# One load of the query weights becomes five strided loads on the sync engine's queue, with the small inputs behind them

## The chip, the core and the metric

The kernel runs on one core of a Trainium2 chip. The core has a matrix engine (PE, its weight loads shown as PEld), a vector engine (DVE), a scalar engine (ACT), GpSimd (POOL) and a sync engine (SP), and sixteen DMA engines that all transfers share. SP and ACT each issue transfers on a queue of their own. The metric is device time in microseconds (us), the median of several executions; lower is better.

## The reference

One decoding step of a transformer layer, two sequences (B = 2), one new token each, width D = 512:

- layer norm of x, then q = norm(x) @ wq, split into H = 32 heads of 128;
- attention of each of the 64 pairs (sequence, head) over 8192 cached keys and values: `softmax(q k^T / sqrt(128)) v`, all in float32;
- the heads' outputs times wo (4096 x 512), added to x;
- a second layer norm, `relu(. @ w1 + b1)**2 @ w2 + b2` with 1792 hidden columns, added again.

The 64 blocks of keys and values are 8.39 MB each and make up 537 of the 561 MB that are read. The query weights wq are another 8.39 MB, wo is 8.39 MB, w1 and w2 are 3.67 MB each. The small inputs (x, b1, b2) are 13 KB.

## The kernel before

All inputs are laid out on the host so that a load is one contiguous row for each of the 128 partitions. The on-chip memory holds `ring`, three slots of 128 partitions x 16384 float32, 64 KB a partition and 8.39 MB a slot. A key and value block fills one slot. Slot 2 first takes the query weights, and later wo; slot 0 takes w1 and w2 at the end.

**Opening.** ACT issues the load of the small inputs into `sm` (line 200) on its own queue; SP issues the query weights into slot 2 (line 201) and then key and value blocks 0 and 1 into slots 0 and 1 (lines 202 and 203). DVE and PE compute the layer norm from `sm` (the reduction `part` at line 253, then `xc`, `rstd`, `xn` up to line 258). PE multiplies `xn` by the weights (lines 269 to 274), `big` is turned and scaled into `QT` (lines 276 to 282), and the first queries are spread into `q3` and `QR`. When PE has read the weights, SP issues block 2 into slot 2 (line 287).

**Loop.** Lines 306 to 313 are SP's loop: for each block, wait until a slot is free, then issue the next load into it. Lines 315 to 350 are the loop of PE, DVE and ACT over blocks 0 to 59: scores on PE, maximum on DVE, exponentials on ACT, four weighted sums on DVE, after which the slot is free.

**Tail.** The last four blocks, wo, w1, w2, the projection and the second half of the layer follow in straight code. The last instruction of weight is the store of `out` (line 591).

**What sets the order.** Outside the loop every operation is recorded by the class `Line` with the memory that it reads and writes, and `plan()` works out which semaphores it must wait for. Three rules of it matter here. First, `region()` (lines 51 to 60) describes an access by the tensor's name and the range of elements *within a partition*; it leaves out which partitions are touched:

```python
lo = ap.offset % row
hi = lo + 1 + sum(step * (n - 1) for step, n in ap.ap[1:])
```

Second, in `plan()` (lines 69 to 80) two accesses conflict when their ranges overlap and one of them is a write. A conflict is passed over when the earlier one has the same engine as `source`, but a load is entered under a name of its own, `("load", n)`, and not under `"sp"`:

```python
if l < hi and lo < h and (w or write):
    if source == engine and (engine == "pe" or not w):
        continue
    needs[source] = max(needs.get(source, 0), n)
```

Third, an operation that needs a load waits on its engine's queue until that load's semaphore has reached 16 (`flush()`, line 118), and what the engine has to issue behind it stands behind that wait. A load issued by SP also waits for the load eight before it (`AHEAD`).

The blocks 0, 1 and 2 are issued by plain operations, which `plan()` doesn't see as writes of the first two slots.

Of the kernel before, what the change touches and what calls it, by code (L numbers as in the profile page):

```python
# [167 lines left out]
def attention_block_kernel(nc, small, kvd, wqd, wod, w1d, w2d, out):  # L168
    def sb(name, *shape):
        return nc.alloc_sbuf_tensor(name, [P, *shape], F32).ap()  # L170

    line = Line(nc)
    pe, dve, act, sp = nc.tensor, nc.vector, nc.scalar, nc.sync
# [5 lines left out]
    ring = sb("ring", SLOTS, ROW)  # L179
# [16 lines left out]
    sm = sb("sm", DB * B + FB + DB)  # L196
    xT = sm[:, : DB * B].rearrange("p (a b) -> p a b", b=B)
    b1T = sm[:, DB * B : DB * B + FB]
    b2T = sm[:, DB * B + FB :]
    line.load(sm, small, "act")  # L200
    line.load(ring[:, 2], wqd)
    for i in range(2):
        line.op("sp", lambda e, i=i: e.dma_start(slot(i), kvd[i]).then_inc(kv_full[i], 16))
    line.op("sp", lambda e: e.sem_inc(s_free, 2))
# [420 lines left out]
```

## Time and profile before

| what | value |
|---|---|
| median of 3 runs (lowest, highest) | 1304.16 us (1303.73, 1304.47) |
| the profiled execution: its time, its span | 1303.86 us, 1302.2 us |
| read from HBM | 561.00 MB, 431 GB/s over the span |
| DVE, PE, ACT busy | 740.4, 417.2, 144.9 us |
| DMA issue of the query weights, to landing | at 0.75 us, 21.9 us |
| DMA issue of the small inputs, to landing | at 0.74 us, 22.1 us |
| first reduction of the small inputs on DVE | at 22.86 us |
| issue of blocks 0 and 1; of block 2 | from 1.20 us; at 35.09 us |

The span is the time from the first to the last instruction; the profiled execution's time is 1.66 us more. A transfer has two times: its issue, an instruction of some 0.4 us on the issuing engine, and its landing, when its semaphore is complete. In the views of transfers a packet is what one DMA engine moves at a stretch; here it is one partition's row of 64 KB, and a slice that shows 9 is one in which packets begin, the whole of a packet being counted where it begins.

### The profile page before, as it was taken

How to read it: one execution, taken by the hardware profiler on the slowest of the kernel's cores; microseconds unless marked ns; L12 is line 12 of the kernel's file. 1: busy time of each engine (PE TensorE's matmuls, PEld its weight loads, DVE VectorE, ACT ScalarE, POOL GpSimd, SP SyncE). 2: the span in 40 equal slices, each digit the busy share in tenths (PEclk: the TensorE clock that was granted, in tenths of full speed). 3: DMA queues.
4: the chain of work that ended last, by engine and by line, in shares of the span. 5: the costliest groups of instructions: out<-in, count | busy, mean ns of one | idle time of the engine just before them, and what ended most of it. 6: DMA issues, size and time to landing. Idle time of an engine off the chain costs nothing. (4 is left out here: it accounts for less than half of the span.)

```text
span 1302.2 us, 6730 instructions
## 1 busy us (share of the span) xinstructions
PE 417.2 (32%) x2438; PEld 112.1 (9%) x2438; DVE 740.4 (57%) x709; ACT 144.9 (11%) x152; POOL 0.7 (0%) x6
## 2 busy tenths in 40 slices
PE   2323223313313313313323323322322332332546
PEld 0100000000000000000000000000000000000112
DVE  0365655665564665665565565665566466556564
ACT  1010111011011011011011011011101001101111
POOL 0000000000000000000000000000000000000000
PEclk9666667566666667666556556656656656655778
DMA  9999999999999999999999999999999999999998
GB/s 419 420 445 425 445 425 443 425 437 433 431 437 427 443 423 445 425 443 427 443 425 435 435 429 439 423 445 425 445 425 443 425 439 431 433 435 427 428 429 367
DMA packets 12104, 561.18 MB, mean 431 GB/s; under 512 B 1472, under 2 KB 1600, under 8 KB 2880
## 3 DMA queue, kind: packets, MB, share of 16 engines
q1 hardware_dynamic: 11952, 561.06, 99.7%
q8 instruction: 5, 0.08, 0.0%
q10 hardware_dynamic: 144, 0.01, 0.0%
q14 instruction: 3, 0.02, 0.0%
HBM read 561.00 MB, written 0.07 MB: 431 GB/s over the span
## 5 line engine op out<-in xcount | busy, mean ns | idle before, releaser
L345 DVE SCALAR_TENSOR_TENSOR ring<-ring,s 128x2048 f32<-128x2048 f32 x240 | 534.7, 2284 | 136.3 <-DVEq L299 136.3
L328 PE MATMUL s<-ring,q 128*32 128x512 f32 x1920 | 354.5, 906 | 800.2 <-PEq L299 800.2
L334 DVE TENSOR_REDUCE st<-s 128x1 f32<-128x2048 f32 x60 | 137.5, 2292 | 330.6 <-DVEq L299 330.6
L340 ACT ACTIVATE s<-s,st 128x2048 f32<-128x2048 f32 x60 | 116.5, 1942 | 1037.1 <-ACTq L299 1037.1
L328 PEld LDWEIGHTS s<-ring,q 128*32 128x32 f32 x1920 | 88.9, 158 | 1064.8 <-issue 1064.8
L155 DVE SCALAR_TENSOR_TENSOR ring<-ring,s 128x2048 f32<-128x2048 f32 x15 | 33.7, 2283 | 6.8 <-ACT s L137 6.8
L133 PE MATMUL s<-ring,QR 128*32 128x512 f32 x128 | 22.1, 851 | 31.4 <-DMA ring<-in_kvd 25.0
L159 DVE TENSOR_REDUCE ALL<-s 128x1 f32<-128x2048 f32 x4 | 9.2, 2292 | 19.2 <-PE s L133 19.2
L345 DVE DVE_READ_ACCUMULATOR ring<-ring,s 128x1 f32 x240 | 19.9, 83 | 0.0
L349 DVE TENSOR_SCALAR ALL<-st 128x6 f32 x60 | 10.3, 171 | 15.1 <-DVEq L299 15.1
L137 ACT ACTIVATE s<-s,ALL 128x2048 f32<-128x2048 f32 x4 | 7.8, 1942 | 49.6 <-DVE ALL L159 49.6
L159 DVE TENSOR_REDUCE part<-sm 128x2 f32<-128x8 f32 x1 | 0.2, 160 | 21.8 <-DMA sm<-in_small 21.8
L340 ACT ACTIVATION_READ_ACCUMULATOR s<-s,st 128x1 f32 x60 | 11.6, 193 | 0.0
L133 PE MATMUL s<-ring,OT 128*2 128x512 f32 (+1 forms) x70 | 9.7, 684 | 3.6 <-DMA ring<-in_wod 3.6
L133 PE MATMUL s<-part,ones_d 128*128 128x2 f32 x8 | 2.1, 332 | 24.2 <-DVE part L159 24.2
L133 PE MATMUL s<-ring,xn 128*2 128x512 f32 x64 | 9.4, 751 | 0.8 <-DVE xn L147 0.8
L133 PEld LDWEIGHTS s<-ring,QR 128*32 128x32 f32 x128 | 4.9, 150 | 47.3 <-DMA ring<-in_kvd 27.0
L133 PE MATMUL s<-lw,pick_all 128*128 128x32 f32 (+2 forms) x6 | 1.9, 395 | 13.7 <-DVE lw L147 13.7
L151 DVE TENSOR_SCALAR QT<-s 128x64 f32<-128x64 f32 x1 | 0.2, 225 | 10.6 <-PE s L133 10.6
L137 ACT ACT_TABLE_LOAD x4 | 5.1, 1283 | 1.2 <-PEq L618 1.2
L133 PE MATMUL s<-ring,xc 128*2 128x448 f32 x32 | 5.0, 739 | 0.4 <-DVE xc L147 0.3
L133 PE MATMUL s<-ring,a 128*2 128x128 f32 x112 | 4.0, 272 | 3.8 <-DMA ring<-in_w2d 3.7
(73 smaller groups left out, 57.5 us busy)
## 6 DMA issues: line engine op xcount, KB each, us to landing
ring<-in_kvd SPq DMA_DIRECT2D x3, 4096.0 KB, 32.6
ring<-in_wod SPq DMA_DIRECT2D x1, 4096.0 KB, 27.5
ring<-in_w1d SPq DMA_DIRECT2D x4, 896.0 KB, 21.5
ring<-in_kvd SPq DMA_DIRECT2D x1, 3072.0 KB, 28.7
ring<-in_wod SPq DMA_DIRECT2D x1, 2048.0 KB, 33.2
ring<-in_w2d SPq DMA_DIRECT2D x2, 1024.0 KB, 15.6
ring<-in_wod SPq DMA_DIRECT2D x1, 1536.0 KB, 36.4
ring<-in_kvd SPq DMA_DIRECT2D x2, 512.0 KB, 37.5
```

The source lines that it names most:

```text
L133: self.op("pe", lambda e: e.matmul(out, lhsT, rhs, start=start, stop=stop), [lhsT, rhs], [out])
L137: self.op("act", lambda e: e.activation(out, in_, func, bias=bias, scale=scale, accum_out=accum_out), [in_, *more], [out] + ([] if accum_o ...
L151: self.op("dve", lambda e: e.tensor_scalar(out, in_, by, None, op0=ALU.mult), [in_, *more], [out])
L155: self.op("dve", lambda e: e.scalar_tensor_tensor(out, a, by, b, op0=op0, op1=op1, accum_out=accum_out), [a, b, *more], [out] + ([] if acc ...
L159: self.op("dve", lambda e: e.tensor_reduce(out, in_, axis=AX.X, op=op, negate=negate), [in_], [out])
L328: made = pe.matmul(bk[n][32 * j : 32 * j + 32, :], q3[:, u, :], keys(u)[:, j, n * BLK : (n + 1) * BLK], start=True, stop=True)
L334: dve.tensor_reduce(nm, s, axis=AX.X, op=ALU.max, negate=True).then_inc(m_full, 1)
L340: act.activation(s, s, AF.Exp, bias=nm, scale=1.0, accum_out=ls).then_inc(e_full, 1)
L345: made = dve.scalar_tensor_tensor(v, v, 1.0, s, op0=ALU.mult, op1=ALU.mult, accum_out=st3[:, u, 2 + e : 3 + e])
L349: dve.tensor_scalar(ALL[:, bass.ds(i0 + u, 1)], st3[:, u : u + 1], 1.0, None, op0=ALU.mult).then_inc(kv_free, 1)
```

## The change

The small inputs are no longer issued by ACT but by SP, behind the query weights. The query weights are no longer one load of 128 partitions but five: partitions 0, 8, 16, ... (16 of them), partitions 4, 12, 20, ... (16), and then three loads of 32 partitions that begin at 1, 2 and 3 and go in steps of 4. Together they are the same 128 rows of 64 KB. Everything else stays.

```diff
-    line.load(sm, small, "act")
-    line.load(ring[:, 2], wqd)
+    for lo, step in ((0, 8), (4, 8), (1, 4), (2, 4), (3, 4)):
+        line.load(ring[lo::step, 2], wqd[lo::step])
+    line.load(sm, small)
     for i in range(2):
         line.op("sp", lambda e, i=i: e.dma_start(slot(i), kvd[i]).then_inc(kv_full[i], 16))
     line.op("sp", lambda e: e.sem_inc(s_free, 2))
```

In the built program the second to the fifth of these loads each carry a wait for the load before them; the load of the small inputs and those of blocks 0 and 1 carry none. PE's first product with the weights waits for the fifth load.

## The prediction

> **What bounds the kernel now.** I read the page's first lines, then busy time and transfers by stretch:
>
> ```profile
> 0.00:22.40 22.40, 0.00 (x0) 0.00 (x0) 0.18 (x3) 3.68 (x4) 0.70 (x6) 1.00 1.01 422
> 22.40:100.00 77.60, 29.12 (x180) 8.81 (x180) 35.69 (x43) 9.12 (x11) 0.00 (x0) 0.71 1.00 430
> 500.00:700.00 200.00, 59.67 (x320) 14.89 (x320) 117.70 (x108) 20.58 (x20) 0.00 (x0) 0.61 1.00 435
> 1278.50:1302.20 23.70, 15.31 (x208) 7.01 (x204) 6.72 (x24) 2.22 (x5) 0.00 (x0) 0.90 0.86 351
> ```
>
> The last two columns are the DMA engines' busy share and GB/s. From the first microseconds to 1278.5 us the share is 1.00, while DVE, the busiest engine, works 118 of 200 us. The transfers bound the kernel, so idle time put into their stream near the start moves everything behind it by as much. The loop can't take it back by waiting less, because SP already waits for slots, in the wait view:
>
> ```profile
> SPq L299 <- SPq L299: 1128.8, 60, 27.3
> ```
>
> Next SP's own instructions in order of time, and the landings in the transfer view of 0 to 25 us:
>
> ```profile
> 0.75 0.39 SPq L130 DMA_DIRECT2D ring<-in_wqd  x1
> 1.20 0.91 SPq L203 DMA_DIRECT2D ring<-in_kvd  x2
> 35.09 0.33 SPq L287 DMA_DIRECT2D ring<-in_kvd  x1
> 63.61 1084.75 SPq L309 DMA_DIRECT2D ring<-in_kvd  x57
> ```
>
> ```profile
> sm<-in_small ACTq DMA_DIRECT2D x1, 13.0 KB, 22.1
> ring<-in_wqd SPq DMA_DIRECT2D x1, 21.9
> ```
>
> Three loads are queued by 2.1 us, so each DMA engine goes from one load to the next without a gap. The weights land at 0.75 + 21.9 = 22.65 us, the small inputs at 22.84.
>
> Now one row. These are the transfer views of 0 to 3 us and of 3 to 6 us (packets, MB, share of the window), and then the slices of 1.6 to 2.4, of 4.6 to 5.6 and of 22.2 to 23.2 us:
>
> ```profile
> q1 hardware_dynamic: 16, 1.05, 103.9%
> ```
>
> ```profile
> q1 hardware_dynamic: 16, 1.05, 80.6%
> ```
>
> ```profile
> DMA  0000000009900999909900000090090000000000
> ```
>
> ```profile
> DMA  0000000009990099090090909099009000000000
> ```
>
> ```profile
> DMA  0990190000000000000000000000000000000000
> ```
>
> A row of 64 KB takes 80.6% of 3 us = 2.42 us on one engine, and the first row of an empty stream 103.9% = 3.12 us, 0.70 more. First rows begin from 1.78 to 2.2 us (1.03 to 1.4 us after the issue), second rows from 4.83 to 5.35. So the slowest engine is done with its first row 4.60 us after the issue. Block 0's rows follow the weights' last ones by 22.33 us at the latest, 0.3 us before the landing.
>
> **The change part by part.** *The loads become a chain.* `region()` gives all five the same range of slot 2, since it leaves partitions out; a load is not entered as "sp", so `plan()` makes each wait for the landing of the one before. Four waits stand in SP's queue, and behind them the remaining weights, the small inputs and blocks 0 and 1: at each the DMA engines run dry. One such boundary, on the slowest engine:
>
> - last row done to landing, 0.3 us (above);
> - landing to the next issue, 0.1 us: in the chain of waits SP takes 0.03 plus 0.04 us after DVE releases it at 1244.24 us; 0 to 0.2;
> - issue to the end of the first row beyond the 2.42 us that the row takes anyway: 4.60 - 2.42 = 2.18 by the first load. The store at the end begins sooner: issued at 1300.60, its first packets are in the 22nd slice of 0.04 us, 0.84 us later instead of 1.03. The loads are of the first load's kind, but the program's first issue is also its coldest (0.39 us against 0.33), so I take 2.0. Low end 0.84, no cold row and no spread; high end 2.18 plus the longest rest of one engine in the trace's packets, 1.2 us before 42.4 us, where the loops are entered.
>
> This makes 2.4 us (1.2 to 3.8), four times 9.6 us (5 to 15). The first load starts as before and behind the last one the stream is full again.
>
> *The loads become narrow.* Every load of the trace has 128 partitions, and its packets run at 2.42 us with sixteen in flight. No row shows sixteen rows of every eighth partition. If the sixteen ways to memory belong to the engines, such a row takes 2.42 us (nothing lost, nothing gained, as bytes and engines stay). If they belong to groups of partitions, two of these rows can share one way, and as the share is already 1.00 a shared way is slower: 2 x 2.42 = 4.84 us. For the loads of 16 rows I take the slow end, though 2.42 is the only row there is: a load of 128 leaves a choice which rows run together, a load of 16 leaves none, and a fixed stride has to suit the grouping exactly to meet sixteen different ways. That is 2 x 2.42 = 4.8 us. For the loads of 32 rows I take the fast end, because each engine has two rows and a finer stride reaches more groups; the slow end is 3 x 4.84 = 14.5 us more.
>
> [...]
>
> *The small inputs change queue.* ACT loses one issue of 0.40 us; its next work from data waits until 24.94 us, so that is worth nothing. SP gains one issue of about 0.4 us before block 0. Cover: the fifth load's two rows, 4.84 us on each engine, hide this issue and block 0's (0.45 us); without them the stream would run dry by 0.8 us. The 128 packets of 104 B ran on the same engines before, between the rows. They now land just behind the weights; before, 0.2 us behind them. So layer norm, product and `QT` (22.86 to 37.2 us) move with the weights' landing, and block 0, whose scores begin at 43.6, moves by the same amount: 6 us of margin stay.
>
> *What is late next.* Nothing more. Block 2 is issued after the product (35.09 us), and needs only to be queued before block 1 is through (about 61 us): 26 us to spare, both moving together. The first load of SP's loop (63.61) has all of block 2 ahead of it. The waits by `AHEAD` begin with the eighth load, and there are six.
>
> *Sum.* 9.6 + 4.8 = 14.4 us onto the profiled execution's 1303.86 (span 1302.2 plus 1.66 around it) is 1318.3. The median shown stands 0.3 us higher, so 1318.6 us. In time: loads issued near 0.75, 8, 15.5, 22.5 and 30 us, the last landing near 37.
>
> **The rivals.**
>
> 1. *Chain only.* The ways belong to the engines; 4.84 us fall away: 1304.16 + 9.6 = 1313.8 (1309 to 1319). For it: 2.42 us in every stretch. Against: none of these rows comes from a strided load.
> 2. *Narrow throughout.* The loads of 32 share ways too: each engine's two rows lie next to each other, so neighbouring engines stay on the same ways. 1318.6 + 14.5 = 1333.1, less if engines drift out of step. For it: a load has no reason to order its rows by way. Against: loads of 128 rows run at full rate, so for those something does.
> 3. *Won back in the loop: not slower.* The delay is 14.4 us; 11.8 of it would have to come back for a time within 0.2%, over the 60 looped blocks, 0.2 us each. A block takes 8 x 2.42 = 19.4 us on an engine, so a row would need 2.39 us, because the engines leave the opening in a better step. Against: the stretches run at 430 to 435 GB/s and share 1.00, and 435 is no more than 0.9% above the mean of 431.
> 4. *Fewer engines.* If a strided load runs on one engine alone, 128 rows x 2.42 = 310 us replace 19.4: near 1600. Nothing in the trace speaks for it; the loads seen use all sixteen.
>
> **How the numbers follow.** Forecast (chain, 16-row loads at half rate) 0.44, with 1314 to 1324 as its own range from the chain's ends; chain only 0.25; narrow throughout 0.23; won back or otherwise not slower 0.03; fewer engines or another delay beyond 1336 us 0.05. The predicted time is the first case's 1318.6. The range leaves out the slowest part of the last cases and the quick end of the second: 1311 to 1334. A difference of 0.2% (2.6 us) is about what a measurement of this kernel tells from none. Slower by more: 0.97, the first three cases and the last; the case of the time won back is split into 0.02 within and 0.01 faster, for which the loop would have to gain 17 us.
>
> **What would show it.** In the changed kernel's wait view, four waits of SP for `ring<-in_wqd`, some 26 us together; blocks 0 and 1 issued after 30 us instead of 1.20; in the transfer views, four stretches without packets of 2 us and more before 37 us, and first packets of about 5.5 us instead of 3.1 in the first two loads (3.1 would be rival 1; 4.84 for rows of 32-row loads rival 2). The loop's and the tail's stretches should be unchanged but for their start, by the same amount as the weights' landing. I am wrong if SP's issues follow each other without waits, or if the total moves by another amount than that landing.

## The result, and the profile after

The changed kernel takes 1320.74 us (1320.65 to 1321.08) against 1304.16 us: 16.6 us or 1.28% slower, ratio 1.0128 with a 95% interval of 1.0116 to 1.0140. The forecast was 1318.6 us with a range of 1311 to 1334. The profiled execution took 1320.65 us over a span of 1319.1 us, so that the two profiled executions are 16.8 us apart, and times read from the traces differ by 16.8 instead of 16.6.

The waits of the sync engine, in the changed kernel (in total, times, longest):

```profile
SPq L300 <- SPq L300: 1128.7, 60, 28.9
SPq L130 <- DMA ring<-in_wqd: 28.7, 4, 7.2
```

The first line is SP's wait for free slots in the loop, the same as before (1128.8 us). The second is new: four waits for the query weights, 28.7 us, 26 us forecast. SP's instructions in order of time, in the changed kernel (start, length), from windows that hold one issue each:

```profile
0.74 0.62 SPq L130 DMA_DIRECT2D ring<-in_wqd  x1
8.48 0.51 SPq L130 DMA_DIRECT2D ring<-in_wqd  x1
16.19 0.49 SPq L130 DMA_DIRECT2D ring<-in_wqd  x1
23.86 0.48 SPq L130 DMA_DIRECT2D ring<-in_wqd  x1
31.60 0.47 SPq L130 DMA_DIRECT2D ring<-in_wqd  x1
32.11 0.59 SPq L130 DMA_DIRECT2D sm<-in_small  x1
32.75 1.00 SPq L204 DMA_DIRECT2D ring<-in_kvd  x2
```

The five loads go out 7.7 us apart whether they hold 16 or 32 rows, and blocks 0 and 1 follow at 32.75 instead of 1.20 us. Busy time and transfers by stretch, in the changed kernel (the last two columns are the DMA engines' busy share and GB/s):

```profile
0.00:39.20 39.20, 0.00 (x0) 0.00 (x0) 0.18 (x3) 3.68 (x4) 0.70 (x6) 1.00 0.73 239
517.00:717.00 200.00, 55.56 (x320) 14.10 (x320) 119.88 (x110) 20.59 (x20) 0.00 (x0) 0.64 1.00 435
1295.30:1319.10 23.80, 17.07 (x212) 8.02 (x204) 7.46 (x24) 2.30 (x5) 0.00 (x0) 0.80 0.85 346
```

The opening runs at 239 GB/s where it ran at 422. The loop runs as it did, at share 1.00 and 435 GB/s, and the tail takes the same 24 us. The delay is made in the first 39 us and carried unchanged to the end: the first reduction of the small inputs starts at 39.68 us instead of 22.86 (16.8 later), the store of `out` is issued at 1317.42 instead of 1300.60 (16.8 later). First the lines of the kernel before, then those of the changed one:

```profile
22.86 0.16 DVE L159 TENSOR_REDUCE part<-sm 128x2 f32<-128x8 f32 x1 [21.84 <-DMA sm<-in_small]
1300.60 0.34 SPq L591 DMA_DIRECT2D out<-res  x1
```

```profile
39.68 0.16 DVE L159 TENSOR_REDUCE part<-sm 128x2 f32<-128x8 f32 x1 [38.65 <-DMA sm<-in_small]
1317.42 0.35 SPq L592 DMA_DIRECT2D out<-res  x1
```

Last, the rows. The transfer views of 1 to 4, 9 to 12, 17 to 20 and 20 to 23 us of the changed kernel hold the rows of the first load, those of the second, and the first and second rows of the third (packets, MB, their time as a share of sixteen engines' 3 us):

```profile
q1 hardware_dynamic: 16, 1.05, 160.6%
```

```profile
q1 hardware_dynamic: 16, 1.05, 162.5%
```

```profile
q1 hardware_dynamic: 16, 1.05, 100.7%
```

```profile
q1 hardware_dynamic: 20, 1.05, 80.7%
```

Sixteen packets are in flight each time (they begin within 1 us of one another), as many as there are engines, but a row of the two 16-row loads takes 160.6% and 162.5% of 3 us, 4.8 and 4.9 us. The first row of a 32-row load takes 3.02 us and its second 2.42, as the rows of the whole load did before. (The four packets more in the last line are under 512 B. Each load of the weights has sixteen such behind its rows.)

### The profile page after: what moved, and what is told of

The parts are those of the page before. It is cut to its first block, busy times and chain, and to the rows that moved or that the text cites. A ratio compares the mean times of both kernels' runs of the same rounds, so it can differ in the third digit from the quotient of the medians.

```text
span 1319.1 us, 6734 instructions
## 1 busy us (share of the span) xinstructions
PE 398.9 (30%) x2438; PEld 109.7 (8%) x2438; DVE 740.3 (56%) x709; ACT 145.1 (11%) x152; POOL 0.7 (0%) x6
## 5 line engine op out<-in xcount | busy, mean ns | idle before, releaser
L329 PE MATMUL s<-ring,q 128*32 128x512 f32 x1920 | 331.9, 854 | 822.7 <-PEq L300 822.7
L329 PEld LDWEIGHTS s<-ring,q 128*32 128x32 f32 x1920 | 84.3, 151 | 1069.5 <-issue 1069.5
L341 ACT ACTIVATION_READ_ACCUMULATOR s<-s,st 128x1 f32 x60 | 11.6, 193 | 0.0
```

The source lines that it names most:

```text
L329: made = pe.matmul(bk[n][32 * j : 32 * j + 32, :], q3[:, u, :], keys(u)[:, j, n * BLK : (n + 1) * BLK], start=True, stop=True)
L341: act.activation(s, s, AF.Exp, bias=nm, scale=1.0, accum_out=ls).then_inc(e_full, 1)
```

## The experiments

The theory: the loss is the sum of two things, a gap of the whole DMA stream at each of four waits, and the two 16-row loads that run on half of the ways into memory. Such ways are the author's assumption; what the views show is the time of a row. The main rivals: narrow or strided loads cost their time in any case, or the small inputs' new queue has a part in it. All differences below are against the runs of the kernel before on the same chip (median 1304.01 us for the five loads without waits, the four chained loads, the halves and the small inputs alone, 1304.09 for the other three).

**The five loads without waits.** `region()` names the partitions too, so that loads of different partitions don't conflict; SP issues all five from 0.75 us on, and PE waits for all of them.

```diff
-        return ap.tensor.name, lo, hi
+        name = ap.tensor.name
+        if name == "ring":
+            first, (step, n) = ap.offset // row, ap.ap[0]
+            return [(f"{name}{p}", lo, hi) for p in range(first, first + n * (step // row), step // row)]
+        return [(name, lo, hi)]
```

> The five loads stay, but the planner now also compares partitions, so the loads no longer wait for one another and SP issues all of them at once. Theory (chain plus shared ways): the four gaps of 2.9 us fall away (7.7 us from issue to issue in the changed kernel less two rows of 2.42), what stays is the sharing in the two loads of 16 rows, at most 2 x 2.42 = 4.8 us: 1304.5 to 1309.5 us, first packets near 4.7 us in the first two rows of each engine. Rival (each narrow load costs its time whether or not it waits): 1320 us as the changed kernel.

Measured: 1309.35 us (1309.18 to 1309.41), ratio 1.0041 (1.0027 to 1.0055), 5.3 us above before. SP's waits for the weights are gone, and with them 11.4 us of the changed kernel's time (1320.74 less 1309.35). The five issues now follow each other within 3.2 us:

```profile
0.75 3.18 SPq L134 DMA_DIRECT2D ring<-in_wqd  x5
```

What is left is in the rows; the transfer views of 1 to 4, 6 to 9 and 14 to 16.5 us, of this kernel:

```profile
q1 hardware_dynamic: 16, 1.05, 162.1%
```

```profile
q1 hardware_dynamic: 32, 1.05, 164.7%
```

```profile
q1 hardware_dynamic: 16, 1.05, 96.9%
```

The first two rows of each engine take 4.86 and 4.94 us (shares of 3 us; the second line counts sixteen packets under 512 B too), the fourth 96.9% of 2.5 us, 2.42. (The third, in the view of 11 to 14 us, takes 2.95.) The chain and the narrow loads are two separate costs.

**Four loads of 32 rows, chained.** The two 16-row loads are joined into one in steps of 4; the waits stay.

```diff
-    for lo, step in ((0, 8), (4, 8), (1, 4), (2, 4), (3, 4)):
+    for lo, step in ((0, 4), (1, 4), (2, 4), (3, 4)):
```

> Four chained loads of 32 rows in steps of 4 instead of five; the two loads of 16 rows are one. Theory: three gaps of 2.9 us and no shared way, 1304.2 + 8.7 = 1313 us (1312 to 1314), each engine's first row near 3.1 us and second 2.42, SP issues 7.7 us apart. Rival (every strided or narrow load is slow, not only those on half the ways): about 2.4 us more for each of four loads, 1322 us.

Measured: 1313.36 us (1313.10 to 1313.38), ratio 1.0072 (1.0056 to 1.0089), 9.35 us for three boundaries, 3.1 us each. By SP's issues (0.74, 8.35, 16.02 and 23.82 us) a boundary is 2.8 to 3.0 us, as in the changed kernel: 7.61 to 7.80 us less two rows of 2.42. The rest is the last load's own later landing (7.7 us after its issue, 2.9 beyond its two rows, where the undivided load landed 2.5 beyond its eight) and the spread between runs. In the second load's first and second rows, in the transfer views of 9 to 12 and 12 to 15 us,

```profile
q1 hardware_dynamic: 16, 1.05, 102.4%
```

```profile
q1 hardware_dynamic: 16, 1.05, 80.6%
```

no row takes twice as long (3.07 and 2.42 us). What is paid is gaps alone.

**The same four loads without waits**, with the `region()` of the first experiment.

> Four loads of 32 rows in steps of 4, without waits for one another. Theory (what is lost is gaps and shared ways, and here there is neither): 1304.2 to 1304.7 us, the later first packet of a strided load (about 0.3 us) being all that stays; the first rows near 3.1 us, the others 2.42. Rival (strided loads share ways by chance whenever they are narrow): 1307 us or more.

Measured: 1304.45 us (1303.98 to 1304.61), ratio 1.0002 (0.9992 to 1.0011): no difference that the runs can tell. Strided loads of 32 rows cost nothing that can be measured when they follow each other without waits. Their first and second rows take 3.21 and 2.44 us, in the views of 1 to 4 and 4 to 7 us:

```profile
q1 hardware_dynamic: 16, 1.05, 107.1%
```

```profile
q1 hardware_dynamic: 16, 1.05, 81.2%
```

Beside the first experiment (1309.35 us), whose loads differ only in that the first 32 rows come as 16 and 16, this puts 4.9 us on the two 16-row loads; 4.8 had been forecast.

**Two halves, and every second partition.** Two chained loads of 64 rows, once of neighbouring partitions, once of every second one.

```diff
+    for lo in (0, 64):
+        line.load(ring[lo : lo + 64, 2], wqd[lo : lo + 64])
```

> Two chained loads of 64 neighbouring partitions, 0 to 63 and 64 to 127. Theory (the ways belong to groups of partitions, and one half of the partitions reaches only half of them): one gap of 2.9 us plus eight rows that take 4.84 instead of 2.42 us, 19.4 us: 1326.5 us (1323 to 1328), packets of 4.84 us throughout the weights. Rival (the ways belong to the engines, and the 16-row loads were slow because a single row per engine is a cold one): one gap alone, 1307 us, packets of 2.42 us after the first.

```diff
+    for lo in (0, 1):
+        line.load(ring[lo::2, 2], wqd[lo::2])
```

> Two chained loads of 64 rows as in the halves, but every second partition (0, 2, 4, ... and then 1, 3, 5, ...) instead of neighbours. Theory (a load is slow when its partitions reach only half of the ways; every second partition reaches all): one gap of 2.9 us, 1304.1 + 2.9 = 1307 us (1306 to 1308), packets of 2.42 us after each load's first. Rival (the sharing comes from loads of fewer than 128 rows being dealt out to the engines in an order that collides): about 1328 us like the halves.

Measured: 1328.07 us (1327.99 to 1328.53), ratio 1.0186 (1.0169 to 1.0203), for the halves; 1307.37 us (1307.13 to 1307.59), ratio 1.0025 (1.0015 to 1.0035), for every second partition. Same engines, same bytes, one wait each, and 20.7 us between them. Every second partition costs 3.3 us, and its rows show nothing but a gap, which was expected at 2.9: SP's two issues (0.75 and 13.42 us) are 12.67 us apart, 3.0 more than four rows, and the second load's own later landing adds 0.2. The transfer views, first of the halves (6 to 9 us), then of every second partition (7 to 9.5 us):

```profile
q1 hardware_dynamic: 16, 1.05, 170.7%
```

```profile
q1 hardware_dynamic: 16, 1.05, 96.8%
```

In the halves each of sixteen packets in flight takes 170.7% of 3 us, 5.12; with every second partition it is 96.8% of 2.5 us, 2.42. So the limit doesn't lie with the engines but with which rows run together, and a row of the halves takes slightly more than twice as long (5.12 against 2 x 2.42 = 4.84 us), which is why the halves end just above the range expected. The rows lie in HBM in the order of their partitions, so a step changes their distance there too. That distance doesn't explain the halves, whose rows lie 64 KB apart like those of the undivided load, while rows 128 KB apart (every second partition) and 256 KB apart (the loads of 32) take 2.42 us. For the 16-row loads (512 KB apart) no run separates the partitions from the source. Sixteen rows of 65,536 B in 5.12 us are 205 GB/s in the halves, in 2.42 us they are 433 GB/s. Why 64 neighbouring partitions are slower is not shown; ways that belong to groups of partitions are the author's explanation.

**Chained, but wide.** Four chained loads of all 128 partitions, each a quarter of the columns, with a conflict noted for the whole slot.

```diff
+    for n in range(NQ):
+        cut = slice(n * ROW // NQ, (n + 1) * ROW // NQ)
+        line.op("sp", lambda e, cut=cut: e.dma_start(ring[:, 2, cut], wqd[:, cut]), [], [ring[:, 2]], load=True)
```

> Four chained loads that each have all 128 partitions and a quarter of the columns (16 KB a row, eight rows an engine, as many bytes a load as four loads of 32 rows). Three gaps with the widest loads. If a gap is longer than the predicted 2.4 us because a narrow, strided load starts later (1.27 us from issue to the first packet in the changed kernel, 1.03 us in the kernel before), the gaps are 2.4 us here: 1311.3 us (1310.5 to 1312). If every chained load has the same gap, 2.9 to 3.1 us: 1313 us or more, as the four loads of 32 rows (1313.36).

Measured: 1310.78 us (1310.59 to 1311.03), ratio 1.0051 (1.0034 to 1.0067), 6.7 us for three boundaries, 2.2 us each (2.3 by SP's issues at 0.75, 7.93, 15.09 and 22.24 us, less 4.84 us of rows): here the forecast's 2.4 holds, and narrow loads have the longer gap. The rows of this kernel are also shorter, 16 KB instead of 64, so width isn't the only difference. Where the difference lies is seen at the third load of this kernel and the fourth of the changed one. SP's issue, then the slices of 15 to 16.5 us, of the wide loads; then the issue and the slices of 23.8 to 25.3 us of the changed kernel:

```profile
15.09 0.33 SPq L202 DMA_DIRECT2D ring<-in_wqd  x1
```

```profile
DMA  0000000000000000000000000000909909999000
```

```profile
DMA  0000000000000000000000000000000000099090
```

A slice is 37.5 ns. The wide load's first packets are in the 29th slice, at 16.05 us, 0.96 after the issue; the narrow load's (issued at 23.86, shown above) in the 36th, at 25.11 us, 1.25 after it. The issue itself takes 0.33 us wide and 0.48 narrow. The stride isn't the reason: the two halves, 64 neighbouring rows each, take 0.57 and 0.47 us to issue (at 0.75 and 23.83), and the first packets of the first are in the slice at 2.05 us of its view of 1 to 4 us, 1.30 after the issue.

**The small inputs alone.** The weights in one load as before, the small inputs behind them on SP's queue.

```diff
-    line.load(sm, small, "act")
     line.load(ring[:, 2], wqd)
+    line.load(sm, small)
```

> The weights in one load as before; only the small inputs move from ACT's queue to SP's, behind the weights. Theory: nothing, 1304.2 us (1303.5 to 1304.9); the small inputs land within 0.3 us of the weights, as before. Rival (the queue of the small inputs carries part of the loss): 1305 us or more.

Measured: 1304.03 us (1303.72 to 1304.59), ratio 1.0000 (0.9991 to 1.0010). The first reduction starts at 23.10 us, 0.2 later than before, and the block that it must be ready for comes 20 us after. The queue of the small inputs has no part in the loss.

## Why the prediction was right

*The bound* held. The loop and the tail were not changed by anything but their start; the delay of the weights' landing (16.8 us, from 22.7 to 39.5) is the delay of the end. Rival 3, the time won back in the loop, is out: 435 GB/s before and after.

*The chain of waits* held as a mechanism: taking the waits away took 11.4 us away. Its size was too small. The sum had 2.4 us a boundary, 9.6 in all. In the changed kernel two issues around a 32-row load are 7.67 and 7.74 us apart; less two rows of 2.42 us that makes 2.9 us a boundary, 11.6 for four. The term that failed is "issue to the end of the first row beyond the 2.42 us", taken as 2.0 us from the first load and the final store, because the program's first issue was thought to be the coldest. Behind a 32-row load SP's next issue follows the last row by 0.3 us (23.55 to 23.86), so the term was 2.9 - 0.3 = 2.6 us. The wide loads show that 2.0 was right for loads of 128 rows; the value was carried over to loads of 16 and 32 rows, which are issued more slowly (0.47 to 0.51 us against 0.33), start 0.3 us later, and take longer from the first packet to the next issue (25.11 to 31.60 us, 6.49, in the fourth load, against 16.05 to 22.24, 6.19, for as many bytes in the third wide one). The boundary's 2.9 us lay within its ends of 1.2 to 3.8.

*The narrow loads*, 4.8 us, held: 4.9 by the two runs without waits. It is met in sum and not row by row. In the run without waits the two slow rows take 4.86 and 4.94 us, 1.7 and 2.5 more than a first and a second row of the kernel before (3.12 and 2.42), and the third row, at 2.95, adds another 0.5. The choice between the ends, the slow one for 16 rows and the quick one for 32, was right on both counts, though the reason given for it, that a fixed stride has to suit the grouping, was only a likelihood. That there are sixteen ways into memory, and that they can belong to groups of partitions, was the author's assumption, and no run shows a way. What the two runs with loads of 64 rows show is that a row takes 5.12 us when the 64 partitions are neighbours and 2.42 when they are every second one. Two details were off. The slow first rows were expected at 5.5 us and are 4.8, no longer than slow rows further on (4.94 without waits, 5.12 in the halves), so the 0.7 us of a cold row doesn't come on top. And behind a 16-row load SP's next issue comes 0.8 us after the last row, not 0.3 (7.68 to 8.48 us), which makes up for it. That the boundary comes to 2.9 us behind both kinds of load is so far a coincidence. The halves have the longer wait too, by an estimate: their last third row begins in the slice at 12.80 us (the view of 11 to 14 us), two rows of 5.12 from there end at 23.0, and the next issue comes at 23.83. So it would go with the slow rows and not with 16 of them; why stays open.

*Rival 1* (chain only) and *rival 2* (narrow throughout) are out by the rows: 4.8 us in the two loads of 16, 2.42 in those of 32. *Rival 4* is out too, as sixteen packets are in flight in every load.

*The small inputs*, costed at nothing, cost nothing. *What is late next*, nothing, also held: `QT` is followed by the queries' copies until 53.4 us, and block 0's scores start at 60.20, 7 us of margin.

The sum in the end, by the changed kernel's own issues: 5.3 + 5.3 us (7.74 and 7.71 less one row) and 2.8 + 2.9 (7.67 and 7.74 less two) make 16.3. The fifth load lands 7.9 us after its issue, 3.1 beyond its two rows, where the undivided load landed 2.5 beyond its eight, and this adds the rest to 16.8. The prediction had put that at nothing. Of the 2.2 us that the forecast's 14.4 fell short of 16.6, the four gaps make 2.0. Four stretches without any packet were expected to be 2 us or more: they are 2.1, 2.1, 1.6 and 1.6 us, as a gap is made of the slowest engine's delay and not only of the time in which all rest.

Four readings of the prediction were off without moving the sum. The view of 1.6 to 2.4 us holds fifteen first rows; the sixteenth begins near 2.95, in the last slice of 0 to 3 us, but the 4.60 us was taken from the second rows. The first issue (0.39 us) isn't the coldest: issues of up to 0.43 us stand in the same trace, so nothing but the store's earlier start spoke for 2.0 instead of 2.18. The high end's rest of 1.2 us isn't idle: four packets of another kind (`instruction`) were moved there, by the view of 38 to 46 us. And a wait by `AHEAD` begins with the ninth load, not the eighth.

No version here beats the kernel before. Without waits and with 32 rows a load it is equalled (1304.45 against 1304.09 us).

## What to carry to other kernels

A planner that describes an access without its partitions turns strided pieces of one load into a chain, and in this kernel, which is bound by transfers (share 1.00 in the loop), each wait of the issuing queue on its own load cost a full stop of the stream: 2.3 us from issue to issue with 128 partitions, 2.8 to 3.0 with fewer. When a load is cut by partitions, look at the duration of its packets: here the rows took 2.42 us behind the first in pieces of every second or fourth partition, but 4.8 to 4.9 us in pieces of every eighth and 5.12 in one half, though sixteen were in flight each time. Where nothing waits for the pieces, leave it whole.

## What was not expected of the hardware

A row takes 5.12 us in the halves, where each engine has four rows in a line; that is more than twice 2.42. A piece of the weights with fewer than 128 partitions takes 1.25 to 1.4 us from its issue to its first packet, against 0.96 to 1.03 with 128, strided or not; the reason wasn't looked for. Its issue takes 0.47 to 0.62 us, against 0.33 to 0.39 for weights of 128 partitions, but the number of partitions isn't all there is to it: the issue of the small inputs, which have 128, takes 0.59 us behind the five pieces and 0.42 behind the undivided load. Loads of 64 and 32 rows in steps of 2 and 4 run at 2.42 us a row, also in the chained runs, where sixteen rows start anew behind each wait: only their first rows are well over 2.42 us (3.0 to 3.2), and about as long as in an undivided load (3.12).
